# A planned two-layer kernel: another price for instruction fetch, and the value weights loaded as two halves

## The chip, the core and the metric

The kernel runs on one core of one Trainium2 chip. A core has five engines that take their instructions in order and meet only at semaphores: TensorE (PE in the profile, its weight loads PEld), VectorE (DVE), ScalarE (ACT), GpSimd (POOL) and SyncE (SP), which here only issues DMAs. The metric is the device time of one execution in microseconds; the time of a kernel is the median of its runs.

## The reference, cut to what matters

The input x is 2048 rows of 512 numbers. Two layers run one after the other, each with the same attention and the same gated block:

```python
def A(x):   # 32 heads of 16, window of 256 keys, no bias
    q, k, v = split(x @ wqkv)
    p = softmax(where(0 <= i - j < 256, q @ k.T * 16 ** -0.5, -1e9))
    return (p @ v) @ wo
def B(x):   # 512 -> 1792 -> 512
    return (sigmoid(x @ w_gate) * (x @ w_up)) @ w_down
x = x + A(layernorm(x)); x = x + B(layernorm(x))
x = x + A(layernorm(x)); x = x + B(layernorm(x))
```

The second layer uses the same weights as the first.

## The kernel before

**Tiles and stages.** The 2048 rows are 16 tiles of 128, in groups of four. For each layer and tile the stages are: layer norm (statistics L649 and L651 on VectorE, the root on GpSimd L662 and L663, the subtract-and-multiply "apply" L681 on VectorE), a transpose of the normalised tile into `xnT` (by TensorE and a copy for the first tiles, L704, otherwise as a DMA transpose of two tiles, L728), the projections of a group (queries L780, keys L811, and per tile the values L847), whose results ScalarE (L738) or VectorE (L740) copies out of a PSUM bank. The keys are then split on VectorE into even and odd halves (L826, two instructions for a quarter of the heads).

**Visits.** Attention goes in 154 visits. A tile has five: four of kind A (one for each quarter of the heads, scores at L1106) and one of kind R for the window's edges (L1117), which stands third and needs all four quarters; the last tile of a layer has two. In each, TensorE writes scores into the one PSUM tile `Sps`, ScalarE takes the exponential of 2048 columns (L1159, 1.88 us) into a ring, and VectorE multiplies masks in (L1037). The next visit's scores cannot start before ScalarE has read `Sps`. When a tile's masks are done, TensorE multiplies the probabilities with the values, in two halves of 80 small matmuls (L1186); their result is moved (L740 or L738), transposed (L1205), divided by the row sums (L1240, L1241), transposed back (L1213), multiplied with wo (L970) and added to x (L976).

**The gated block.** It works in chunks of 1, 2 or 4 tiles given by the list `GLU`: gate and up matmuls of 128, 256 or 512 columns (L875), a tanh on ScalarE (L893), a product on VectorE (L901), then 14 matmuls a tile for the down projection (L939) and the add (L948). For layer 1 the rows then go out (L955).

**What sets the order.** No scheduler of the framework is at work: class `Plan` is a list scheduler that runs while the program is built. It keeps a clock, a queue of ready tasks for VectorE, ScalarE, GpSimd and SP, and TensorE's clock; whatever the plan starts next is written next into that engine's program. Its prices are constants: a matmul of n columns takes n/2.4 + 2.5 ns, an exponential 1880, a change between kinds of matmul 100. `ARRIVE` and `RATE` say when the first loads land and how fast the later ones flow. `Plan.held` and `Plan.issue` count TensorE's instructions: for every 256 a new line is fetched, and a line is usable `LINE_NS` after the previous one was entered; when TensorE would come sooner, the plan holds it. Among several ready tasks an engine takes the one with the smallest `prio`; `rank` chooses TensorE's next unit of dense work; `pace` is the least planned time from one visit to the next. Before the change `prio`, the DMA slack, the ranks and the pace come from one table, `SEGMENTS`, with a new entry every five visits or so.

The method `pick` takes TensorE's next step: values if the plan is in them, a visit's scores if they are due, otherwise a step of a dense unit (L1338).

**The first loads.** SP and ScalarE each issue half of the first x tiles and half of the key and query weights. Then:

```python
weights("k", 1)
weights("q", 0)
self.has_wq["v"] = at("v", [first(self.wq[:, :, 2 * D:3 * D], wq_src[:, :, 2 * D:3 * D], "ACT")])
x_group(1)
self.has_wo = load(self.wot[:], wo_src, D * D * 2)
```

So the value weights go out as one DMA of 512 KB on ScalarE's queue, and x tiles 4 to 7 as two DMAs of 256 KB on SP's, beside each other. Until the first weights are there, TensorE is kept busy with dummy matmuls (L1370).

Of the kernel before, what the change touches and what calls it, by code (L numbers as in the profile page):

```python
# [12 lines left out]
P = 128  # L13
# [43 lines left out]
def pool_ns(n):  # L57
# [5 lines left out]
GLU = [[[1, 1, 1, 1, 2, 2], [1, 1, 1, 1, 2, 2], [1, 1, 2, 2, 2], [1, 1, 1, 1, 1, 1, 1, 1], [2, 2, 2, 2], [1, 1, 2, 1, 1, 2], [2, 2, 4]], [[4, 4, 4, 2, 2], [4, 4, 4, 2, 2], [4, 4, 2, 2, 4]]]  # L63
EARLY = 16
# [5 lines left out]
ARRIVE = dict(x0=3280, x1=4280, x2=5600, k=8560, q=10000, v=10900)  # L70
# [3 lines left out]
RATE = ((10900, 40.0), (1e9, 345.0))  # L74
# [3 lines left out]
LINE_NS = 3550  # L78
# [3 lines left out]
OPT = dict(gu='SP', g1=1, bk=3, bq=2, wide=0, r0=2, g0=5, g2=0, x0=1, eps=1, hold=1, own=1, ck=0, cq=2, turn=2,  # L82
    split=0, mo=0, at=3, r1=1, near=1)
RANK = dict(x3=31008.59915082838, wd=1355.5443193096523)


class Late(dict):


    def __missing__(self, name):  # L90
        return {"vv": self["v"], "tp": 0, "tp_g": 2}[name] if name in ("vv", "tp", "tp_g") else self[name[:-1]]


SEGMENTS = {
    0: (False, dict(st_x0=16.387, ap_x0=6.225, xt_x0=7.482, st_x1=3.545, ap_x1=7.915, xt_x1=12.783, st_x=12.637,
        ap_x=12.681, xt_x=-4.829, st_p=-0.616, ap_p=7.606, xt_p=5.184, st_g=-0.445, ap_g=2.621, xt_g=-2.868,
        st_g0=3.679, ap_g0=-17.463, xt_g0=-4.767, tp=8.093, tp_g=6.212, q=-2.808, q0=10.418, q1=-21.607, k=-11.975,
        k0=12.49, k1=0.894, s=-4.824, s0=2.968, s1=4.16, v=-0.758, v0=18.344, v1=21.96, vv=-1.006, exp=-7.486,
        exp0=-1.374, m0=3.414, m00=5.808, e0=-7.871, e00=2.35, e1=1.881, e10=8.977, m2=1.191, m20=5.467, th=14.916,
        mu=-10.778, dn=-19.706, add=-0.599, add0=7.919, out=-15.994, mv=30.614, mv0=7.196, oq=-9.099, oq0=-8.293,  # L100
        no=9.304, no0=-3.84, on=10.221, on0=-11.559, vc=9.867, vc0=-2.298), dict(xt=3835, oq=509, on=2499, vc=2407),
        dict(tp=-26.503, o=-3.164, lead=15.979, far=73.841, v=2.438, g=58.124, d=37.228, feed=44.486,
        x3=31008.59915082838, wd=1355.5443193096523, go=147.94192547482436), 1500.53),
    5: (False, {}, {}, {}, 1500.53),
    10: (False, {}, {}, {}, 1500.53),
    15: (False, {}, {}, {}, 1500.53),
    16: (False, {}, {}, {}, 1690.96),
    20: (False, {}, {}, {}, 1690.96),
    25: (False, {}, {}, {}, 1690.96),
    26: (True, dict(st_p=1.672, ap_p=36.822, xt_p=-2.918, st_x=-11.841, ap_x=0.6, xt_x=14.582, st_g=-13.947,  # L110
        ap_g=-7.573, xt_g=7.949, q=-14.515, k=21.982, s=1.709, v=-1.564, exp=-39.767, m0=2.485, e0=7.8, e1=8.391,
        m2=14.841, th=1.045, mu=-20.576, dn=-2.4, add=-13.535, out=27.454, mv=35.926, oq=-4.313, no=8.505, on=12.109,
        vc=-17.889), dict(xt=240, oq=3128, on=2754, vc=10020), dict(tp=36.947, o=-40.166, lead=9.199, far=17.491,
        v=-2.507, g=13.193, d=13.247, feed=-46.58, go=607.5028023985727), 2727.3),
    30: (False, dict(ap_x=1.293, dn=-2.072), dict(oq=2609), dict(feed=-47.788), 2681.58),
    35: (False, dict(st_p=0.51, ap_g=-7.3, mu=-24.39), dict(oq=2664, on=2941), dict(o=-39.26, lead=12.63, go=494),
        2681.58),
    40: (False, dict(st_p=1.672, ap_g=-7.573, mu=-20.576), dict(xt=779, oq=2609, on=2754), dict(o=-40.166,
        lead=9.199, go=607.5028023985727), 2620.7),
    45: (False, dict(st_p=0.82), dict(xt=240), dict(g=8.75, go=213), 1879.3),  # L120
    50: (False, dict(st_p=1.672), {}, dict(g=13.193, go=607.5028023985727), 2681.58),
    55: (False, {}, dict(xt=86), dict(lead=13.76), 2574.1),
    60: (False, {}, dict(xt=240), dict(lead=9.199), 2681.58),
    65: (False, {}, {}, {}, 2681.58),
    70: (False, {}, {}, {}, 2764.0),
    75: (False, {}, {}, {}, 2681.58),
    80: (False, {}, {}, {}, 2717.8),
    85: (False, dict(k=22.27, e0=8.47), {}, dict(far=18.98, v=-3.32, g=13.07), 2632.8),
    90: (False, dict(q=-15.93, k=21.982, e0=7.8, e1=11.21, add=-11.69), dict(on=2458), dict(lead=9.39, far=17.491,
        v=-2.507, g=14.8), 2717.8),  # L130
    95: (False, dict(q=-14.515, e1=8.391, add=-13.535), dict(on=2754), dict(lead=9.199, g=13.193), 2717.8),
    100: (False, {}, {}, {}, 2717.8),
    105: (False, {}, {}, {}, 2717.8),
    110: (False, {}, {}, {}, 2717.8),
    115: (False, {}, {}, dict(go=877), 2868.0),
    120: (False, {}, {}, dict(go=607.5028023985727), 2717.8),
    125: (False, {}, {}, {}, 2717.8),
    130: (False, {}, {}, {}, 2717.8),
    135: (False, {}, dict(oq=2597), dict(lead=8.49, far=16.64), 2717.8),
    140: (False, {}, dict(oq=2609), dict(lead=9.199, far=17.491), 2717.8),  # L140
    145: (False, {}, {}, {}, 2717.8),
    150: (False, {}, {}, {}, 2717.8),
}


def segments():

    out, now = {}, [Late(), {}, {}, 0]
    for slot, (new, prio, slack, rank, pace) in SEGMENTS.items():
        now = [Late(prio) if new else Late({**now[0], **prio}), {**now[1], **slack}, {**now[2], **rank}, pace]  # L150
        out[slot] = now
    return out
# [259 lines left out]
def mm_ns(n):  # L412
    return n / 2.4 + 2.5


class Net:


    def __init__(self, ctx, tc, A_x, wqkv, wo, w_gate, w_up, w_down, out):
# [39 lines left out]
        self.slot = 0  # L459

# [30 lines left out]
    def loads(self, A_x, wqkv, wo, w_gate, w_up, w_down):  # L491
# [56 lines left out]
        self.has_wq["v"] = at("v", [first(self.wq[:, :, 2 * D:3 * D], wq_src[:, :, 2 * D:3 * D], "ACT")])  # L548
# [195 lines left out]
    @property  # L744
    def prio(self):
        return self.tables[0]

    @property
    def slack(self):
        return self.tables[1]  # L750

    @property
    def ranks(self):
        return self.tables[2]

    def enter(self, slot):
        self.slot = slot
        if slot in self.segments:
            self.tables = self.segments[slot]
# [11 lines left out]

    def q_unit(self, L, g, cq, i0, n):
# [6 lines left out]
        def steps(bank):  # L779
            return [(mm_ns(w), lambda kt=kt, o=o: nc.tensor.matmul(  # L780
                self.banks[bank][:, o:o + w], lhsT=self.wq[:, kt, cq * P:cq * P + P],
                rhs=self.xnT[key][0][:, i0 + o // P:i0 + (o + w) // P, kt, :],
                start=kt == 0, stop=kt == KT - 1)) for o in range(0, n * P, w) for kt in range(KT)]
# [19 lines left out]
    def k_unit(self, L, g, cq, i0, n):  # L803
# [6 lines left out]
        def steps(bank):  # L810
            return [(mm_ns(w), lambda kt=kt, o=o: nc.tensor.matmul(  # L811
                self.banks[bank][:, o:o + w], lhsT=self.wq[:, kt, D + cq * P:D + cq * P + P],
                rhs=self.xnT[key][0][:, i0 + o // P:i0 + (o + w) // P, kt, :],
                start=kt == 0, stop=kt == KT - 1)) for o in range(0, n * P, w) for kt in range(KT)]
# [27 lines left out]
    def v_unit(self, L, t):  # L842
# [3 lines left out]
        def steps(bank):  # L846
            return [(mm_ns(D), lambda kt=kt: nc.tensor.matmul(  # L847
                self.banks[bank][:], lhsT=self.xnT[key][0][:, t % NBG, kt, :], rhs=self.wq[:, kt, 2 * D:3 * D],
                start=kt == 0, stop=kt == KT - 1)) for kt in range(KT)]
# [17 lines left out]
    def glu_units(self, L, t0, n, c0):  # L867
# [5 lines left out]
        def mms(bank, wts, fcs):  # L873
            pt = self.banks[bank][:, 0:len(wts) * len(fcs) * w].rearrange("p (i f w) -> p i f w", i=len(wts), w=w)
            return [(mm_ns(w), lambda i=i, j=j, fc=fc, wt=wt, kt=kt: self.nc.tensor.matmul(  # L875
# [52 lines left out]
    def down_units(self, L, t, t0, n, c0):  # L928
# [4 lines left out]
        def unit(o, w):  # L933
# [3 lines left out]
            def mm(bank, fc):  # L937
                at = (c0 * GW + fc * n * P + (t - t0) * P) % (HCH * GW)
                nc.tensor.matmul(self.banks[bank][:, 0:w], lhsT=self.hT[:, at:at + P], rhs=self.wd[:, fc, d],  # L939
                                 start=fc == 0, stop=fc == FC - 1)  # L940
                if t == t0 + n - 1 and end:
                    pl.at(pl.pe_free + PE_LATENCY, self.h_used[L, t0, fc].fire)
# [23 lines left out]
    def oproj_unit(self, L, t, b):  # L966
        nc, pl = self.nc, self.pl

        def steps(bank):
            return [(mm_ns(D), lambda c=c: nc.tensor.matmul(  # L970
# [312 lines left out]
    def pick(self):  # L1283
# [23 lines left out]
        if visit and pl.mode == "pv" and go <= 0:  # L1307
            if go > 0:
                return False
# [6 lines left out]
        if visit and (wait <= 0 or go <= 0 and u is None):  # L1316
            self.last_s = pl.now
            end = pl.matmul("s", self.scores(*visit))
# [5 lines left out]
            self.enter(self.slot + 1)  # L1324
# [14 lines left out]
        pl.count(1)  # L1339
        end = pl.matmul("d", ns)  # L1340
# [8 lines left out]

    def do_values(self, pv, spare):  # L1350
        pl = self.pl
        self.pv_list.pop(0)
        bank = min(spare, key=lambda i: self.bank_turn[i])
# [20 lines left out]
    def pace(self, s):  # L1374
        return self.tables[3] if s < len(self.visits) else 0
# [111 lines left out]
    def go(self, *srcs):  # L1487
        pl = self.pl
        self.visit_list()
        self.segments = segments()  # L1490
        self.enter(0)
# [23 lines left out]
        self.v_needs = [self.visit_needs(*v) for v in self.visits]  # L1515
        self.last_s = -1e9
# [80 lines left out]
```

## Time and profile before

| | us |
|---|---|
| median of 3 runs | 540.27 (539.95 to 540.88) |
| the profiled execution: its time | 541.94 |
| the profiled execution: its span | 540.2 |
| PE busy | 523.8 (97% of the span), 9606 matmuls recorded |
| PE weight loads busy | 292.6 (54%) |
| VectorE busy | 417.6 (77%) |
| ScalarE busy | 385.0 (71%) |
| GpSimd busy | 43.5 (8%) |
| DMA of data issued by SP: share of the 16 engines | 31.9% |
| mean granted TensorE clock | 1.00 |

The span is the stretch from the first to the last instruction of the profiled execution; its time has some more around it. Busy times overlap, since the engines work beside each other. A row of the groups or of the timeline names line, engine, operation and tiles; a bracket or an arrow tells how long the engine stood idle before it and what ended that. The chain follows the instruction that ended last back to what released it, step by step. The program has 9674 matmuls; some of them are missing in the records.

### The profile page before, as it was taken

Reading aid. Unit: us, or ns where it says so; the run is one execution under the profiler, and the core shown is the slowest. Engines: PE = TensorE matmul, PEld = TensorE weight load, DVE = VectorE, ACT = ScalarE, POOL = GpSimd, SP = SyncE. Lnnn points to the kernel's source line nnn. Section 1 sums busy time; section 2 is a strip of 40 time slices with the busy share of each in tenths; the row PEclk is TensorE's granted clock in tenths of the full one; section 3 lists DMA queues with packets and bytes.
Section 4 is the critical chain, followed back from the end, with each engine's and each line's share of the span. In section 5 each row is a group of like instructions: output and inputs, shape, how many; then the busy total and the mean of one; then the engine's idle time right before and its main releaser. Section 6 shows DMA issues by size and latency. Waiting matters only on the chain.

```text
span 540.2 us, 21309 instructions
## 1 busy us (share of the span) xinstructions
PE 523.8 (97%) x9606; PEld 292.6 (54%) x9674; DVE 417.6 (77%) x841; ACT 385.0 (71%) x384; POOL 43.5 (8%) x99
## 2 busy tenths in 40 slices
PE   8899999999999999999999998999999999999997
PEld 8446855758657544544444444444444454445873
DVE  6999989898798897779896988789886774442442
ACT  4999988979889797789688887688877751220330
POOL 4411200000001010000110100100000000000000
PEclk9999999999999999999999999999999999999999
DMA  8851433234223327225235325342143224101001
GB/s 261 311 155 52 81 82 42 59 68 80 43 52 42 72 41 93 46 59 72 47 51 72 51 54 48 65 60 63 32 81 52 51 42 69 39 1 38 3 11 39
DMA packets 95067, 36.23 MB, mean 67 GB/s; under 512 B 78336, under 2 KB 93952, under 8 KB 94976
## 3 DMA queue, kind: packets, MB, share of 16 engines
q1 hardware_dynamic: 93600, 33.56, 31.9%
q8 instruction: 75, 1.23, 1.0%
q10 hardware_dynamic: 1376, 1.31, 0.8%
q14 instruction: 16, 0.13, 0.1%
HBM read 9.70 MB, written 2.10 MB: 22 GB/s over the span
## 4 chain that ended last, share of the span: by engine, by line
PE 86%; DMA 4%; DVE 4%; ACT 3%; issue 2%; ACTq 0%; SPq 0%; DVEq 0%
PE bank L875 34%; PE bank L939 17%; PE bank L1186 9%; PE Sps L1106 7%; PE bank L970 5%; PE bank L847 4%; PE bank L811 4%; PE bank L780 4%; DMA xnT<-xn 2%; PE Sps L1117 2%; DMA xsb<-in_A_x_dram 1%; ACT edge L1159 1%; DMA wq<-in_A_wqkv_dram 1%; ACT PTring L1159 1%; DVE st L649 0%
## 5 line engine op out<-in xcount | busy, mean ns | idle before, releaser
L1159 ACT ACTIVATE PTring<-Sps 128x2048 bf16<-128x2048 f32 (+1 forms) x122 | 226.1, 1853 | 45.3 <-PE Sps L1106 41.8
L875 PE MATMUL bank<-xnT,wu 128*128 128x512 bf16 (+2 forms) x728 | 128.6, 297 | 0.1
L875 PE MATMUL bank<-xnT,wg 128*128 128x512 bf16 (+2 forms) x728 | 127.8, 298 | 0.2 <-issue 0.2
L901 DVE SCALAR_TENSOR_TENSOR hT<-hT,bank 128x256 bf16<-128x256 bf16 (+1 forms) x154 | 80.7, 538 | 50.8 <-ACT hT L893 26.3
L893 ACT ACTIVATE hT<-bank 128x256 bf16<-128x256 f32 (+1 forms) x154 | 71.4, 483 | 68.1 <-PE bank L875 67.0
L939 PE MATMUL bank<-wd,hT 128*128 128x512 bf16 (+2 forms) x429 | 101.8, 372 | 3.2 <-issue 2.4
L875 PEld LDWEIGHTS <-wg 128*128 128x128 bf16 x728 | 61.2, 98 | 37.4 <-issue 2.7
L875 PEld LDWEIGHTS <-wu 128*128 128x128 bf16 x728 | 61.9, 98 | 34.6 <-issue 1.9
L939 PEld LDWEIGHTS <-hT 128*128 128x128 bf16 x462 | 42.5, 98 | 47.0 <-issue 1.9
L1159 ACT ACTIVATE edge<-Sps 128x2048 bf16<-128x2048 f32 (+1 forms) x32 | 56.6, 1770 | 13.9 <-PE Sps L1117 13.4
L1186 PE MATMUL bank<-PTring,Vaug 128*32 128x64 bf16 (+1 forms) x2880 | 51.8, 203 | 1.4 <-issue 1.4
L1186 PEld LDWEIGHTS <-Vaug 128*32 128x32 bf16 x2880 | 44.1, 97 | 13.0 <-issue 11.2
L1037 DVE TENSOR_TENSOR PTring<-PTring,mask 128x1024 bf16<-128x1024 bf16 x64 | 43.6, 684 | 7.8 <-ACT PTring L1159 7.7
L740 DVE CAST OTs<-bank 128x512 bf16<-128x512 f32 x52 | 37.8, 728 | 14.0 <-PE bank L1186 13.8
L1106 PE MATMUL Sps<-qT,kTp 32*128 32x256 bf16 (+3 forms) x1216 | 47.4, 248 | 0.8 <-ACT edge L1159 0.4
L649 DVE BATCH_NORM_STATS2 st<-xsb 128x6 f32<-128x512 bf16 x64 | 44.0, 687 | 2.5 <-DMA xsb<-in_A_x_dram 1.8
L1186 PE MATMUL bank<-edge,Vl 128*32 128x64 bf16 x1024 | 44.6, 193 | 0.0
L662 POOL TENSOR_SCALAR st<-st 128x2 f32<-128x2 f32 (+1 forms) x33 | 11.2, 339 | 412.6 <-DVE st L651 412.6
L1106 PEld LDWEIGHTS <-kTp 32*128 32x128 bf16 x1216 | 17.8, 92 | 43.0 <-issue 40.9
L1037 DVE TENSOR_TENSOR edge<-edge,maske 128x1024 bf16<-128x1024 bf16 x60 | 39.9, 681 | 1.2 <-ACT edge L1159 1.0
L1186 PE MATMUL bank<-edge,Vh 128*32 128x64 bf16 x896 | 40.7, 193 | 0.0
L1037 DVE TENSOR_TENSOR PTring<-PTring,maskn 128x1024 bf16<-128x1024 bf16 x56 | 38.2, 682 | 1.7 <-ACT PTring L1159 1.7
(75 smaller groups left out, 523.3 us busy)
## 6 DMA issues: line engine op xcount, KB each, us to landing
Vl<-Vaug SPq DMA_DIRECT2D x32, 68.0 KB, 2.4
out_dram<-xsb SPq DMA_DIRECT2D x15, 128.0 KB, 2.1
Vh<-Vaug SPq DMA_DIRECT2D x28, 68.0 KB, 2.3
wg<-in_B_w_gate_dram SPq DMA_DIRECT2D x2, 896.0 KB, 10.1
wu<-in_B_w_up_dram SPq DMA_DIRECT2D x2, 896.0 KB, 10.7
wd<-in_B_w_down_dram SPq DMA_DIRECT2D x7, 256.0 KB, 3.2
xsb<-in_A_x_dram SPq DMA_DIRECT2D x6, 256.0 KB, 7.2
wq<-in_A_wqkv_dram SPq DMA_DIRECT2D x2, 256.0 KB, 4.7
```

The lines of the kernel that those rows point to most:

```text
L649: nc.vector.bn_stats(out=st[:, 0:6], in_=self.xsb[:, t, :])
L740: self.nc.vector.tensor_copy(out=out, in_=in_)
L780: return [(mm_ns(w), lambda kt=kt, o=o: nc.tensor.matmul(self.banks[bank][:, o:o + w], lhsT=self.wq[:, kt, cq * P:cq * P + P], rhs=self.xn ...
L875: return [(mm_ns(w), lambda i=i, j=j, fc=fc, wt=wt, kt=kt: self.nc.tensor.matmul(pt[:, i, j, :], lhsT=wt[:, kt, fc * P:(fc + 1) * P], rhs= ...
L893: self.nc.scalar.activation(out=self.hT[:, ch[0] * GW:ch[0] * GW + size], in_=pt, func=AF.Tanh, scale=0.5)
L901: self.nc.vector.scalar_tensor_tensor(out=h, in0=h, scalar=1.0, in1=pt, op0=ALU.add, op1=ALU.mult)
L939: nc.tensor.matmul(self.banks[bank][:, 0:w], lhsT=self.hT[:, at:at + P], rhs=self.wd[:, fc, d], start=fc == 0, stop=fc == FC - 1)
L970: return [(mm_ns(D), lambda c=c: nc.tensor.matmul(self.banks[bank][:], lhsT=b[0][:, c, :], rhs=self.wot[:, c, :], start=c == 0, stop=c == ...
L1037: done = pl.task({"DVE": dve_bf_ns(1024)}, lambda e: nc.vector.tensor_tensor(out=r, in0=r, in1=m.to_broadcast([P, 16, HP]), op=ALU.mult), ...
L1106: nc.tensor.matmul(self.sps[:, m, o:o + n * HP], lhsT=kTp[32 * m:32 * m + 32, i, tt, e, :], rhs=self.qT[32 * m:32 * m + 32, i, q0:q0 + n * ...
L1159: nc.scalar.activation(out=out, in_=src, func=AF.Exp, scale=scale)
L1186: nc.tensor.matmul(o, lhsT=Va[:, c0:c0 + 32], rhs=p(h), start=k == 0 or t == 0, stop=k == len(parts) - 1 or t == 0, tile_position=(0, 32 * g))
```

## The change

The prices that the planner reckons with are changed: `LINE_NS` from 3550 to 4500, the planned arrival of v from 10.9 to 11.9 us, of x2, k and q by 0.04 to 0.1 us, and the moment from which later loads flow from 10.9 to 11.6. The table by segments is replaced by two sets of priorities, slacks and ranks with other values: one up to visit 24, one from there on. The pace becomes 1514 ns for the first 16 visits, 56 up to visit 24, then 2675 in layer 0 and 2422 in layer 1 (before: 1501, then 1691, then mostly 2682 and 2718). Two entries of `GLU` change: the chunks of layer 0 are tiles 0, 1, 2-3, 4-5, 6-7, 8-11, 12-15 (before, 4 and 5 stood alone), and layer 1 has four chunks of four (before, the last four tiles were 2 and 2).

The value weights are loaded as two halves of 256 KB, one on ScalarE's queue and one on SP's, and the SP half stands ahead of the x group. A helper `mm` issues most matmuls; it can split one into four column strips, which `OPT["col"] = 0` switches off.

Since the planner makes every engine's order anew from these numbers, the order of the instructions differs on all engines from about the first scores on. TensorE has 9450 matmuls instead of 9674, all of the difference in gate and up. SP has one DMA more. VectorE's and ScalarE's work is the same but for the gated block's chunks and for which of the two makes a copy.

```diff
-GLU = [[..., [1, 1, 2, 1, 1, 2], [2, 2, 4]], [[4, 4, 4, 2, 2], [4, 4, 4, 2, 2], [4, 4, 2, 2, 4]]]
+GLU = [[..., [1, 1, 2, 2, 2], [2, 2, 4]], [[4, 4, 4, 4], [4, 4, 4, 4], [4, 4, 4, 4]]]
+PACE = [2674.92, 2421.83, 1514.06, 55.78, 24.82]
...
-ARRIVE = dict(x0=3280, x1=4280, x2=5600, k=8560, q=10000, v=10900)
+ARRIVE = dict(x0=3280, x1=4280, x2=5500, k=8600, q=9900, v=11900)
...
-RATE = ((10900, 40.0), (1e9, 345.0))
+RATE = ((11600, 40.0), (1e9, 345.0))
...
-LINE_NS = 3550
+LINE_NS = 4500
...
-SEGMENTS = {
...
-}
+PRIO = dict(st_x0=11.96, ap_x0=1.481, xt_x0=15.743, st_x1=4.799, ap_x1=4.987, xt_x1=17.198, st_x=11.858,
...
+SLACK = dict(xt=4114, oq=705, on=2212, vc=3028)
...
+LATE_PRIO = dict(st_p=1.209, ap_p=39.706, xt_p=-8.546, st_x=-19.015, ap_x=12.134, xt_x=28.172,
...
+LATE_SLACK = dict(xt=145, oq=2215, on=3133, vc=11347)
...
-        self.has_wq["v"] = at("v", [first(self.wq[:, :, 2 * D:3 * D], wq_src[:, :, 2 * D:3 * D], "ACT")])
+        weights("v", 2)
...
+    def mm(self, out, lhsT, rhs, start, stop):
+        if not self.col:
+            self.nc.tensor.matmul(out, lhsT=lhsT, rhs=rhs, start=start, stop=stop)
+            return
...
     def pace(self, s):
-        return self.tables[3] if s < len(self.visits) else 0
+        if s >= len(self.visits):
+            return 0
+        if s < PACE[4]:
+            return PACE[2 if s < EARLY else 3]
+        return PACE[self.visits[s][0]]
```

The halves come from a function that was there for the key and query weights:

```python
def weights(name, i):
    h = slice(i * D, i * D + D)
    self.has_wq[name] = at(name, [first(self.wq[:, k:k + 2, h], wq_src[:, k:k + 2, h], q) for k, q in ((0, "ACT"), (2, "SP"))])
```

## The prediction

> **What bounds the kernel now.** I read the page's busy times and chain first, then the chain in order of time, the waits, and the timeline of the first 75 us.
>
> ```profile
> span 540.2 us, 21309 instructions
> PE 523.8 (97%) x9606; PEld 292.6 (54%) x9674; DVE 417.6 (77%) x841; ACT 385.0 (71%) x384; POOL 43.5 (8%) x99
> ...
> PE 86%; DMA 4%; DVE 4%; ACT 3%; issue 2%; ACTq 0%; SPq 0%; DVEq 0%
> ```
>
> TensorE is busy for 97% of the span and is 86% of the chain: the order of its instructions is the time, plus whatever it waits. The chain in order of time gives the prices:
>
> ```profile
> 57.19 2.45 PE bank L875 x42
> ...
> 64.84 0.81 PE bank L1186 x80
> ...
> 283.13 4.55 DMA xnT<-xn
> ...
> 336.26 1.35 issue
> ...
> 352.98 5.01 DMA xnT<-xn
> ...
> 465.41 3.45 PE bank L875 x16
> ...
> 497.78 3.49 PE bank L875 x32
> ```
>
> So a matmul of 512 columns costs 216 ns (3.45/16), of 256 columns 109 (3.49/32), of 128 some 57 (2.45/42), a half of the values 0.81 us; a visit's scores cost 0.33 us (chain pieces at L1106). Where a run of wide matmuls ends and scores or values begin, start to start is 312 ns instead of 216: 0.1 us a change. Adding these up in the order of the built program gives 526.9 us. The span has 13.3 us more: 3.8 by the first scores (12.96 in the trace, 9.2 in the sum), 3.2 behind the last matmul (the last stretch, from 530.0, has 6.95 us of PE), and 6.3 of waits between. Those 6.3 are all that a better order can win. Where they lie:
>
> ```profile
> 14.11 0.69 DVE L649 BATCH_NORM_STATS2 st<-xsb 128x6 f32<-128x512 bf16 x1 [0.82 <-DMA xsb<-in_A_x_dram]
> ...
> 18.15 1.58 DVE L826 TENSOR_SCALAR kTp<-kTp,rm 128x512 bf16<-128x512 bf16 x4
> ...
> 19.78 0.33 PE L1117 MATMUL Sps<-qT,kTp 32*128 32x64 bf16 x20 [0.66 <-DVE kTp L826]
> ```
>
> ```profile
> 59.57 0.41 PE L1117 MATMUL Sps<-qT,kTp 32*128 32x64 bf16 x32
> ...
> 60.06 1.88 ACT L1159 ACTIVATE edge<-Sps 128x2048 bf16<-128x2048 f32 x1
> ...
> 61.99 0.40 PE L1106 MATMUL Sps<-qT,kTp 32*128 32x256 bf16 x8 [0.40 <-ACT edge L1159]
> ```
>
> The first shows VectorE idle for 0.82 us until the second group of x is there, and TensorE then waiting for VectorE's key splits (with the wait at 18.91, 1.24 us). The second shows the exponential's cycle: scores at 59.57, ScalarE until 61.94, next scores at 61.99, so 2.42 us from visit to visit at the least. At visit 22 (72.8 us) the trace is 7.1 us behind the sum, 3.3 more than at the first scores; from there to the end only 2.9 are added: 1.35 at 336.26 inside one run of values ("issue": nothing the profile shows), about 1.1 at the two DMA pieces above, the rest in tenths.
>
> **The change, part by part.** (1) *TensorE's own work.* Tiles 4 and 5 of layer 0 go from two chunks of one tile to one of two, tiles 12 to 15 of layer 1 from 2+2 to 4. The first trades 224 matmuls of 128 columns for 112 of 256: 112 x (2x57 - 109) = -0.5 us. The second trades 224 of 256 for 112 of 512: 112 x (2x109 - 216) = -0.2. The order has 379 runs instead of 374, five more changes at 0.1: +0.5. Dummy matmuls are 80 in both. The helper that now issues the matmuls has its split switched off. Sum -0.2 us.
>
> (2) *The head.* SP issues one more DMA (about 0.65 us, the spacing of its neighbours) ahead of the x group, so both x halves, the output weights and all behind them go out one place later. Before, the two x halves landed at 10.6 and 14.0 and the whole value block on ScalarE's queue at 14.5 (issued at 4.20, 10.3 us to landing). TensorE's first value matmul is at 17.11, so the earlier value weights win nothing. x is now last of the same bytes on the same DMA engines: I put it at 14.0 to 14.5, take 14.35, +0.3. The Trainium skill, "DMA: Bandwidth & Descriptors", section "Issuing engines are not separate DMA queues", says that DMAs issued by several engines run on the same 16 DMA engines and that a second queue saves only issue time, which speaks against this part; v and x landing half a microsecond apart agree with it, and by it x comes no sooner and the sum is 542.2 us, where halves at twice the rate would make it 539.5.
>
> What matters more: in VectorE's new order the statistics of tiles 4 and 5 (which wait for x) stand ahead of the second key split, where before they stood behind it. Visit 1 needs that split. By rows: statistics from 14.44, 1.71 us for two tiles (14.11 to 15.82 before), split 0.81 (1.62 for two), so visit 1's scores start at 17.0, not 15.46: 1.5 us late. Everything on TensorE stands behind them: the first transposes of tile 4, the last keys, the values. Then VectorE does an apply 0.4, statistics 0.87, an xnT copy 0.41, a split 0.81 and a qT copy 0.68, until 20.15; the first value unit wants that copy's bank, and TensorE would be there at 18.9: 1.3 more, together 2.8. In exchange visit 2 (R) stands one unit further back, and its 1.24 us of waits at 18.91 and 19.78 go; its lag behind the sum becomes 6.65 instead of 5.5. Net +1.2 us. Ends: x at 12.5 takes both waits away and leaves the gain, -1.5; x at 15.0 gives +1.9.
>
> (3) *Visits too close together.* Between successive scores the new order leaves 1.74, 2.17, 1.98 and 1.75 us of TensorE's work (visits 4, 7, 9, 15); the cycle is 2.42: 0.68 + 0.25 + 0.44 + 0.67 = 2.0 us of waits. Before there were 2.29 and 1.95: 0.6. Net +1.4; ends 0 (other waits fall into the same gaps) and +2.0.
>
> (4) *Hand-over between stages.* From the last down matmul of a group to its first queries the chain by rows is: matmul 0.38, add 0.69, statistics 0.69 + 0.18, GpSimd 0.34 + 0.76, apply 0.81, DMA transpose 3.7 (median) to 5.0: 7.5 to 8.9 us. For tiles 8 to 11 before layer 1's queries the new order has 7.5 us of work between (14.4 before), so 0 to 1.4, take 0.6; for the gate work of tiles 8 to 11 in layer 0 it has 8.3 (9.5), take 0.3. For tiles 12 to 15 it has 16.4 (12.6), so the wait at 358 goes. Set against the 1.1 that the trace has now: -0.2; ends -1.1 and +2.0.
>
> (5) *Instruction fetch.* The planner now counts 4,500 ns for 256 instructions. The trace's instruction packets come 3.5 us apart at the closest and TensorE stood 1.35 us once. But the new order has as many places as the old one where two value halves stand back to back (three runs of 160), the densest there are. So I give half of the 1.35 back: -0.7; ends -1.4 and +1.4. The Trainium skill, "Runtime: NRT & Kernel Launch", section "Instruction fetch mechanics", calls the cost of crossing a 16 KiB block mostly hidden; by it this term is 0 and the sum 0.7 higher.
>
> (6) *Closer visits in layer 1.* Most stand 2.54 to 2.60 us apart (2.76 to 2.81 before), with one gap of 14.2 that is full of gate and down work. VectorE is 85% busy there now (42.4 of 50 us from 350 to 400) and has 7% less time per visit; late masks would hold the values up. +0.4; ends 0 and +2.0.
>
> Sum: -0.2 + 1.2 + 1.4 - 0.2 - 0.7 + 0.4 = +1.9 us on the profiled execution, whose time was 541.94 for a span of 540.2; the median is 1.67 below it, so 540.27 + 1.9 = 542.2 us.
>
> **Rivals.** *x lands early.* By the trace's packets 15 of the 16 parts of v were through by 11.9 us and one lagged until 14.0. If the halves spare x that laggard, VectorE never waits for it and the head is -1.5 instead of +1.2: 542.2 - 2.7 = 539.5, not slower. It decides from the point where x lands more than 1.5 us earlier than before. Against it: the load and the laggard are the same. *Close visits are free.* ScalarE is 96% busy from 30 to 45 us and may be the bound there in both orders, so that the gaps of TensorE's work below 2.42 us cost nothing: 542.2 - 1.4 = 540.8, no change. For it: ScalarE's total work is nearly the same. Against it: TensorE idles only 0.6 us of the 30 from 30 to 60, so its own work sets the pace now. With both, 538.1: faster. *Much slower.* Layer 1 has no slack: four groups whose transposes take 5.0 instead of 3.7 us, and values that wait for masks, 4 x 1.3 less the 1.3 counted: 542.2 + 3.9 = 546.1. For it: both transposes on the chain took 4.55 and 5.01; against: the gap of 14.2. *The change doesn't do what it says*: the longer fetch shows nowhere in the density, so (5) gives nothing back: 542.9, inside the likeliest's range.
>
> **How the numbers follow.** Likeliest 0.48 (540.8 to 544.5 by its own), x early alone 0.10, close visits free alone 0.11, both 0.12, much slower 0.19. Below 538.6 and above 546.0 I leave a tenth each. What a measurement can tell is 0.2%, 1.1 us: faster is below 539.2, slower above 541.35. Faster is both (0.12) and the lower part of x early: 0.15. Same is the rest of these two and the lowest part of the likeliest: 0.20. Slower is what is left, 0.65.
>
> **What would show it.** In the new profile: VectorE idle for over 1 us before the first statistics of tile 4 near 14.4; scores of visit 1 near 17.0; a wait of the first value unit for a qT copy near 20; scores waiting for the exponential some 0.4 to 0.7 us about visits 5, 10 and 16; visit 22 near 75 us. PE busy within 1 us of 523.8. At 290 to 300 us a wait for xnT under 1.5 us. It is wrong if x lands early, if one wait above 2 us stands in layer 1, or if the run of values at 336 has more than one successor.

## The result, and the profile after

The changed kernel takes 542.2 us (median of 7 runs, 541.58 to 542.85); the kernel before, on the same chip, 540.49 (7 runs, 539.95 to 540.96). The ratio is 1.0025 with a 95% interval of 1.0015 to 1.0034: slower by a quarter of a per cent, 1.7 us. The forecast was 542.2. The number fits, its terms don't: the terms added 1.6 us too much to the time of the profiled execution (541.94 + 1.9 = 543.8, the new profile's is 542.25), and the last step, from the profile down to the median, took off as much too much. That they cancel is luck.

The page of the changed kernel, its span, busy times and chain by engine:

```profile
span 540.5 us, 20853 instructions
...
PE 525.2 (97%) x9382; PEld 280.2 (52%) x9450; DVE 413.9 (77%) x828; ACT 383.9 (71%) x369; POOL 42.7 (8%) x99
...
PE 86%; DVE 7%; ACT 4%; issue 2%; DMA 1%; POOL 0%; ACTq 0%
```

TensorE is still 97% busy and 86% of the chain. The chain of the kernel before had 4% DMA and 4% DVE, this one has 1% and 7%. The share of DVE is no loss by itself: the fastest kernel of this study (run 9 below) has 7% there too. The chain in order of time of the changed kernel, from 285 to 375 us, shows the two pieces that answer to the DMA and "issue" pieces shown for the kernel before:

```profile
294.98 3.08 DMA xnT<-xn
...
321.36 0.52 issue
```

One transpose on the chain instead of two, and 0.52 us in which TensorE waited for nothing that the profile shows, instead of 1.35. So far this is what was forecast. The head is not. The timeline of the changed kernel, first 21 us:

```profile
12.65 0.69 DVE L608 BATCH_NORM_STATS2 st<-xsb 128x6 f32<-128x512 bf16 x1
...
14.27 0.71 DVE L788 TENSOR_SCALAR kTp<-kTp,rm 128x512 bf16<-128x512 bf16 x2
...
15.78 0.40 PE L1068 MATMUL Sps<-qT,kTp 32*128 32x256 bf16 x8
...
18.53 1.67 PE L728 MATMUL bank<-wq,xnT 128*128 128x512 bf16 x6 [0.71 <-DVE qT L699]
...
20.13 0.41 PE L1079 MATMUL Sps<-qT,kTp 32*128 32x64 bf16 x32
```

The statistics of tile 4 start at 12.65 with no idle time before them: x was there already. The second key split comes at 14.27 and visit 1 at 15.78, not at 17.0. The wait for the qT copy is where it was expected, but 0.71 us long instead of 1.3. From then on the close visits show, in the timeline of the changed kernel from 24 to 58 us:

```profile
27.68 0.40 PE L1068 MATMUL Sps<-qT,kTp 32*128 32x256 bf16 x8 [0.57 <-ACT PTring L1121]
...
41.51 0.40 PE L1068 MATMUL Sps<-qT,kTp 32*128 32x256 bf16 x8 [0.54 <-ACT PTring L1121]
...
43.21 0.40 PE L663 MATMUL bank<-ident,xn 128*128 128x128 bf16 x4 [0.33 <-DVE xn L640]
...
56.09 0.40 PE L663 MATMUL bank<-ident,xn 128*128 128x128 bf16 x4 [0.24 <-DVE xn L640]
...
57.02 0.21 PE L1148 MATMUL bank<-PTring,Vaug 128*32 128x64 bf16 x4 [0.30 <-DVE PTring L999]
```

Scores wait for the exponential at visits 5 and 10 (27.68 and 41.51), as forecast. Behind visit 10 (43.21) and ahead of visit 16 (56.09 and 57.02) TensorE waits for VectorE's apply and mask, which was not forecast.

The measure used below is the *lag* of the prediction: the start of a visit's scores in the trace, less the sum of the rows of TensorE's program up to it (the row "sum of rows" is worked out from the prediction's prices and the built program, not measured). The kernel before has two columns, since the fourth run profiled it once more; the fifth and sixth column are two experiments told below (runs 9 and 10).

| lag, us | before, as predicted from | before again | after | chunks alone | chunks and close visits |
|---|---|---|---|---|---|
| visit 0 | 3.79 | 4.30 | 4.11 | 3.90 | 3.92 |
| visit 3 | 5.75 | 5.02 | 5.01 | 4.61 | 4.63 |
| visit 22 | 7.05 | 6.40 | 8.34 | 5.99 | 7.94 |
| last matmul | 9.81 | 8.55 | 9.74 | 6.57 | 9.25 |
| sum of rows | 526.92 | 526.92 | 526.84 | 526.86 | 526.85 |
| from there to the end of the span | 3.47 | 3.46 | 3.88 | 3.45 | 3.46 |

### The profile page after: what moved, and what is told of

Its sections match the earlier page's. It is cut to its first block, busy times and chain, and to the rows that moved or that the text cites. A ratio compares the mean times of both kernels' runs of the same rounds, so it can differ in the third digit from the quotient of the medians.

```text
span 540.5 us, 20853 instructions
## 1 busy us (share of the span) xinstructions
PE 525.2 (97%) x9382; PEld 280.2 (52%) x9450; DVE 413.9 (77%) x828; ACT 383.9 (71%) x369; POOL 42.7 (8%) x99
## 3 DMA queue, kind: packets, MB, share of 16 engines
q8 instruction: 74, 1.21, 1.0%
## 4 chain that ended last, share of the span: by engine, by line
PE 86%; DVE 7%; ACT 4%; issue 2%; DMA 1%; POOL 0%; ACTq 0%
PE bank L728 68%; PE bank L1148 8%; PE Sps L1068 6%; ACT PTring L1121 2%; PE Sps L1079 2%; ACT edge L1121 1%; PE bank L1338 1%; DVE PTring L999 1%; DVE kTp L788 1%; DVE st L608 1%; DVE edge L999 1%; DVE qT L699 1%; DMA xnT<-xn 1%; DVE kTp L699 0%; DVE xsb L938 0%
## 5 line engine op out<-in xcount | busy, mean ns | idle before, releaser
L728 PE MATMUL bank<-xnT,wu 128*128 128x512 bf16 (+2 forms) x616 | 125.0, 321 | 0.0
L855 ACT ACTIVATE hT<-bank 128x512 bf16<-128x512 f32 (+1 forms) x140 | 69.6, 513 | 72.4 <-PE bank L728 71.6
L863 DVE SCALAR_TENSOR_TENSOR hT<-hT,bank 128x512 bf16<-128x512 bf16 (+1 forms) x140 | 78.7, 575 | 52.2 <-PE bank L728 42.7
L728 PE MATMUL bank<-wd,hT 128*128 128x512 bf16 (+2 forms) x427 | 103.2, 372 | 3.2 <-issue 2.2
L728 PEld LDWEIGHTS <-wu 128*128 128x128 bf16 x616 | 54.5, 98 | 40.9 <-issue 2.7
L728 PEld LDWEIGHTS <-wg 128*128 128x128 bf16 x616 | 53.6, 98 | 41.5 <-issue 2.3
L728 PE MATMUL bank<-xnT,wq 128*128 128x512 bf16 (+1 forms) x316 | 63.2, 339 | 0.3 <-DMA xnT<-xn 0.3
L699 DVE CAST OTs<-bank 128x512 bf16<-128x512 f32 x45 | 32.6, 728 | 13.4 <-PE bank L1148 13.4
```

The costliest lines, as they stand in the source:

```text
L699: self.nc.vector.tensor_copy(out=out, in_=in_)
L728: self.nc.tensor.matmul(out, lhsT=lhsT, rhs=rhs, start=start, stop=stop)
L855: self.nc.scalar.activation(out=self.hT[:, ch[0] * GW:ch[0] * GW + size], in_=pt, func=AF.Tanh, scale=0.5)
L863: self.nc.vector.scalar_tensor_tensor(out=h, in0=h, scalar=1.0, in1=pt, op0=ALU.add, op1=ALU.mult)
```

## The experiments

**1 and 2: the halves, undone and alone.** TensorE's order is the same in each pair, so only the loads differ.

```diff
 (1, from the changed kernel; 2 is the reverse in the kernel before)
-        weights("v", 2)
+        self.has_wq["v"] = at("v", [first(self.wq[:, :, 2 * D:3 * D], wq_src[:, :, 2 * D:3 * D], "ACT")])
```

> The changed kernel with the value weights loaded as one block of 512 KB on ScalarE's queue again, everything else as changed; TensorE's order is the same instruction for instruction. Theory (the halves brought x early): the first statistics of tile 4 fall back from 12.65 to about 14.1 us with VectorE idle over 1 us, visit 1 starts near 17 instead of 15.78, visit 2 is over 1 us later, and the time rises from 542.2 to 543 to 544 us. Rival (x's landing has nothing to do with the halves, a lagging DMA engine comes and goes by itself): statistics of tile 4 below 13 us, visit 1 at 15.8, time 542.2.

> The kernel before with the value weights as two halves, nothing else; TensorE's order is that of the kernel before. Theory: x lands near 12.6 us, VectorE's idle 0.82 us at 14.11 and some of TensorE's 1.24 us of waits for key splits at 18.91 and 19.78 go; the lag behind the sum of rows at visit 3 falls from 5.75 to 4.5 to 5.2 us and the time from 540.5 to 539.3 to 540.0. Rival (the key splits wait for something else than VectorE's place behind the statistics): waits unchanged, 540.5.

Run 1: 542.59 us, ratio to the kernel before 1.0038 (1.0024 to 1.0051), beside 1.0025 (1.0015 to 1.0034) with halves: the intervals overlap. Its timeline:

```profile
12.69 0.69 DVE L608 BATCH_NORM_STATS2 st<-xsb 128x6 f32<-128x512 bf16 x1
```

Statistics at 12.69, no idle time, visit 1 at 15.77: x is as early with one block as with halves. The rival holds. Run 2: 541.1 us, ratio 1.0007 (0.9998 to 1.0015): the halves win nothing in the old order either, though in its profile, too, the waits for key splits are down from 1.24 us to one of 0.44 at 18.89.

The fourth run says why: most of that wait was not the order's.

**4: the kernel before, profiled again.** No edit.

> The kernel before, unchanged, profiled once more. Theory (the 1.35 us in which TensorE stood inside a run of values at 336 us belongs to that one execution): no gap over 1 us there, a span near 538.8 us, a time of 540 to 541. Rival (it belongs to the order): 1.2 to 1.5 us at the same place, and a span near 540.

540.68 us, span 538.9. From its timeline, two rows of the head and two of the late part:

```profile
13.72 0.69 DVE L649 BATCH_NORM_STATS2 st<-xsb 128x6 f32<-128x512 bf16 x1
...
19.08 0.33 PE L1117 MATMUL Sps<-qT,kTp 32*128 32x64 bf16 x20 [0.21 <-ACT qT L738]
...
287.28 0.61 PE L780 MATMUL bank<-xnT,wq 128*128 128x512 bf16 x2 [0.92 <-DMA xnT<-xn]
...
336.46 0.21 PE L1186 MATMUL bank<-PTring,Vaug 128*32 128x64 bf16 x2 [0.64 <-issue]
```

In the head the statistics follow without idle time, and of the 1.24 us of waits 0.21 are left, for a copy by ScalarE (in runs 2 and 6, of the same order, one wait for a key split of 0.44 and 0.43 us stays). The late x belonged to the one execution that the prediction was worked out from: there the second half of x tiles 4 to 7 landed at 14.02 us, in 12 others of the 14 profiles of this study at 11.68 to 12.85 (in run 2 it isn't recorded), and it is the only one in which VectorE waits over 0.2 us there. The theory on the stall at 336 us, however, falls: it is there again, 0.64 us long. In the profiles of runs 2 and 6, which have the same order, it is 1.08 and 1.10. It belongs to the order, with a length that varies.

**3: the changed kernel with the early tables of the kernel before.**

```diff
-ARRIVE = dict(x0=3280, x1=4280, x2=5500, k=8600, q=9900, v=11900)
+ARRIVE = dict(x0=3280, x1=4280, x2=5600, k=8560, q=10000, v=10900)
-RATE = ((11600, 40.0), (1e9, 345.0))
+RATE = ((10900, 40.0), (1e9, 345.0))
-PACE = [2674.92, 2421.83, 1514.06, 55.78, 24.82]
+PACE = [2674.92, 2421.83, 1500.53, 1690.96, 24.82]
-SLACK = dict(xt=4114, oq=705, on=2212, vc=3028)
+SLACK = dict(xt=3835, oq=509, on=2499, vc=2407)
...
```

(PRIO and RANK likewise take the values of the first segment of the kernel before.)

> The changed kernel with the planner's early set (priorities, slacks, ranks, arrivals and pace up to visit 24) of the kernel before; halves, chunks, fetch price and the set from visit 24 on stay as changed. TensorE's order up to visit 17 is then that of the kernel before; its rows sum to 527.2 instead of 526.8. Theory (the change loses in the first 75 us, where visits stand closer than the exponential's 2.42 us): the shortfalls up to visit 24 go from 2.1 to 0.4 us, the lag at visit 22 from 8.34 to 6 to 7 us, and the time to 540 to 541. Rival (the loss lies in layer 1, in its closer visits or in the hand-over between stages): lag at visit 22 smaller, but the end no earlier, 542 us.

540.37 us, ratio 0.9995 (0.9986 to 1.0004): the loss is gone. The lag at visit 22 is 5.98 instead of 8.34. TensorE's waits from 20 to 73 us (engine and line, what it waited for: us in total, times, longest), first of the changed kernel:

```profile
PE Sps L1068 <- ACT PTring L1121: 1.1, 2, 0.6
PE bank L663 <- DVE xn L640: 0.6, 2, 0.3
PE bank L728 <- issue: 0.3, 2, 0.2
PE bank L1148 <- DVE PTring L999: 0.3, 1, 0.3
PE Sps L1068 <- ACT edge L1121: 0.2, 1, 0.2
```

and of the third run:

```profile
PE bank L728 <- issue: 0.5, 3, 0.2
PE Sps L1068 <- ACT PTring L1121: 0.3, 1, 0.3
PE Sps L1068 <- ACT edge L1121: 0.2, 1, 0.2
PE bank L1215 <- DVE OTs L699: 0.2, 1, 0.2
```

The waits for ScalarE fall from 1.3 to 0.5 us, those for VectorE from 0.9 to 0.2.

**5 and 6: a shorter exponential in visits 10 to 23**, in the changed kernel and in the kernel before, to see how much of the loss is ScalarE's cycle.

```diff
-        x = pl.task({"ACT": EXP_NS}, lambda e: self.exp(L, t, kind, i), ...
+        x = pl.task({"ACT": EXP_NS}, lambda e: self.exp(L, t, kind, i, 10 <= s < 24), ...
...
+        if short and kind == "A":
+            out, src = out[:, 0:6], src[:, 0:6]
+        elif short and kind == "R" and t > 2:
+            out, src = out[:, :, 0:1], src[:, :, 0:1]
         nc.scalar.activation(out=out, in_=src, func=AF.Exp, scale=scale)
```

> The changed kernel with a shorter exponential in visits 10 to 23: six of eight heads of a kind-A visit, one edge of two of a kind-R visit from tile 3 on (the rest is left out, so part of the attention isn't computed; four small memsets on GpSimd stand in); TensorE's order is the same. Theory (scores wait for ScalarE to have read the score tile where visits stand closer than the exponential's cycle): the cycle falls from 2.42 to about 2.0 us, the 0.9 us lost between visits 15 and 16 (1.75 us of work between them) fall to 0.2 to 0.3, lag growth from visit 10 to 22 falls from 1.5 to about 0.8 us, time 541.4 to 541.8. Rival (the loss there is VectorE's masks or copies, which are the same): growth stays 1.5, time 542.2.

> The kernel before with the same shorter exponential in visits 10 to 23. Theory: only the gap between visits 17 and 18 (1.95 us of work) is below the cycle, so 0.4 to 0.5 us are won; lag growth from visit 10 to 22 falls from 0.9 to 0.4 or 0.5; time 540.6 to about 540.2. Rival: growth stays 0.9 and the time 540.6.

Run 6: lag growth from visit 10 to 22 is 0.56 instead of 0.90, the wait before visit 18 is gone, 540.3 us: ratio 0.9993 (0.9984 to 1.0002). The profile shows what the theory had; the time alone can't tell it from no gain. Run 5: 542.51 us, ratio 1.0036 (1.0023 to 1.0048); lag growth 1.28 instead of 1.50, where the theory wanted 0.8. Between visits 15 and 16 0.79 us are still lost of 0.89. From its timeline:

```profile
55.91 1.45 ACT L1127 ACTIVATE PTring<-Sps 128x1536 bf16<-128x1536 f32 x1 [0.58 <-PE Sps L1070]
...
57.31 0.22 PE L1154 MATMUL bank<-PTring,Vaug 128*32 128x64 bf16 x4 [0.30 <-DVE PTring L1001]
```

ScalarE is done at 57.36 now, and idles 0.58 us before; TensorE stands behind VectorE all the same, in the middle of the values, for a mask. So the theory fails for visit 16. For visits 5 and 10 it rests on the waits in the timeline alone: run 5 leaves the exponentials ahead of them as they were, and the wait at visit 10 stays 0.54 us. Where visits stand close, VectorE's work for them stands close too, and at visit 16 it was VectorE that ended the wait.

**8: the old price for instruction fetch.**

```diff
-LINE_NS = 4500
+LINE_NS = 3550
```

> The changed kernel with the planner's price for a line of TensorE's instructions back at 3,550 ns; TensorE's order up to visit 19 is the same, later parts differ, the rows sum to 527.17 instead of 526.84. Theory (the price buys nothing on the chip, the 1.35 us stall of the kernel before was one execution's): lag at the end 9.5 to 10.0 us as now, the time 0.3 us longer by the sum, 542.2 to 542.6. Rival (the higher price prevents stalls): one or more stalls of 1 to 1.5 us inside a run of values, time 543 to 545.

542.17 us, ratio 1.0021 (1.0012 to 1.0029), beside 1.0025 with the new price. The price is worth nothing that can be measured, and the stall of TensorE is there with both: 0.52 us at 321.88 in the changed kernel (0.53, 0.31 and 0.66 in runs 1, 5 and 11, which have its order), 0.38 at 321.24 here.

**9 and 10: the chunks alone in the kernel before, and with them the close visits.** Run 10 adds to run 9 the changed early set (PRIO, SLACK, RANK, ARRIVE, RATE and the pace up to visit 25).

```diff
 (9)
-GLU = [[..., [1, 1, 2, 1, 1, 2], [2, 2, 4]], [[4, 4, 4, 2, 2], [4, 4, 4, 2, 2], [4, 4, 2, 2, 4]]]
+GLU = [[..., [1, 1, 2, 2, 2], [2, 2, 4]], [[4, 4, 4, 4], [4, 4, 4, 4], [4, 4, 4, 4]]]
```

> The kernel before with the changed chunks of the gated block alone (layer 0: tiles 4 and 5 together; layer 1: four chunks of four). TensorE's order up to visit 24 is that of the kernel before, the rows sum to 526.86 (526.92 before), SP has 328 instructions as before. Theory (the chunks are worth nothing but their rows): 540.4 to 540.9. Rival (fewer, wider matmuls ease the fetch or the hand-over between stages): 539.0 to 539.8.

> The run before this one with the changed early set (priorities, slacks, ranks, arrivals, pace up to visit 25) put into the kernel before, the value weights still one block; TensorE's order up to visit 18 is then that of the changed kernel, later parts are those of the old tables; rows sum to 526.85, SP has 331 instructions. Theory (the changed kernel loses in its first 75 us): lag at visit 22 of 8.2 to 8.6 instead of 6.4, and a time 1.3 to 2.0 us above the run with the chunks alone. Rival (the early loss is made up later, since the late part has slack): within 0.5 us of it.

Run 9: 539.38 us (538.66 to 539.76), ratio 0.9976 (0.9966 to 0.9986). It beats both kernels, by 1.0 and 2.8 us. The theory fails, its rival holds. TensorE's longest waits in it:

```profile
PE bank L939 <- issue: 2.2, 14, 0.2
PE bank L1370 <- DVE hT L565: 1.0, 1, 1.0
PE bank L970 <- issue: 0.5, 3, 0.2
PE Sps L1106 <- ACT edge L1159: 0.4, 1, 0.4
```

and in the kernel before, fourth run, with the two entries that run 9 has no more:

```profile
PE bank L780 <- DMA xnT<-xn: 0.9, 1, 0.9
PE bank L1186 <- issue: 0.6, 1, 0.6
```

The wait for `xnT` at 287 us and the stall at 336 are both gone, and no other took their place. That these two are worth the whole 1.0 us is read from the profile, not shown by a run of its own: the chunks change the order of everything behind visit 24.

Run 10: 541.9 us, ratio 1.0028 (1.0016 to 1.0040). The early set alone costs 2.5 us against run 9. The lag grows by 3.31 us from visit 3 to 22 (3.33 in the changed kernel) instead of 1.38, and nothing of it comes back later. Run 3 takes the set away from the changed kernel and wins 1.8 us (542.2 to 540.37). Together they settle that the changed kernel loses by its early set, most of it ahead of visit 22; which of the set's constants do it, pace or priorities, wasn't tried.

**7, 11 and 12: the end of SP's program.** The changed kernel takes 0.4 us longer from its last matmul to the end of the span, in runs 1, 3, 5 and 8 as well. All of these have 341 to 343 instructions on SP. Run 7 is run 3 with the last stores on another engine, run 11 is the changed kernel with those of four earlier tiles there, run 12 is run 7 with the old fetch price.

```diff
 (7; in 11: nc.scalar if 8 <= t < 12)
-                    pl.dma(640, P * w * 2, lambda: nc.sync.dma_start(out=dst, in_=self.xsb[:, t, d]), ...
+                    pl.dma(640, P * w * 2, lambda: (nc.scalar if t >= 12 else nc.sync).dma_start(out=dst, in_=self.xsb[:, t, d]), ...
```

> The changed kernel with the early set of the kernel before (as in the third run), and the output stores of tiles 12 to 15 issued by ScalarE instead of SyncE, which takes SP from 341 instructions to 331; TensorE's order is that of the third run. Theory (SP stands for some 0.36 us at one fixed instruction, about the 336th of its program, which the kernel before with 328 never reaches): the stretch from the last matmul to the end of the span falls from 3.97 to 3.4 to 3.6 us, the time from 540.4 to about 540.0, below the kernel before. Rival (the tail hangs on the stores themselves): 3.9 us and 540.4, or more, if a store from ScalarE lands later.

> The changed kernel with the output stores of tiles 8 to 11 issued by ScalarE; those of the last four tiles stay on SP. TensorE's order is the same; SP has 335 instructions instead of 343. Theory (SP stands at one fixed instruction of its program near the end): the stretch from the last matmul to the end of the span falls from 3.88 to about 3.5 us, the time by 0.3 to 0.5 us, to 541.7 to 541.9. Rival (in the earlier run the stores on ScalarE did it): 3.9 us and 542.2.

> Early set and fetch price of the kernel before, halves, chunks and late set as changed, the last four tiles' stores on ScalarE (SP 334 instructions). Rows sum to 526.85, 0.3 less than in the run with the early set and the stores. Theory: 539.7 to 540.1, 0.4 to 1.0 below the kernel before. Rival (what the sum gains, other waits take): 540.1 to 540.6.

| kernel | SP instructions | last matmul to end, us |
|---|---|---|
| before, runs 4, 6, 9 | 328 | 3.45 to 3.47 |
| run 2 | 329 | 3.52 |
| runs 10, 7, 12, 11 | 331, 331, 334, 335 | 3.46, 3.54, 3.56, 3.52 |
| runs 3, 1 | 341, 342 | 3.97, 3.90 |
| after, runs 5, 8 | 343 | 3.88, 3.89, 3.90 |

There is a step between 335 and 341 instructions, and it doesn't matter which stores were moved: run 11 keeps the last ones on SP. Run 7: 540.09 us, ratio 0.9993 (0.9984 to 1.0001), beside 0.9995 in run 3; run 11: 541.62, ratio 1.0022 (1.0013 to 1.0031), beside 1.0025. The tail shows the step clearly, the times only lean the same way.

The traces show where it comes from. In the changed kernel SP stands 0.33 us between its 335th and its 336th recorded instruction (539.25 to 539.58 us; two of its 343 are not recorded). In runs 1, 3, 5 and 8 it stands 0.33 to 0.36 us at the very same count, though in run 3 other instructions are there, and the programs with at most 335 end before it.

Whether a fetch of instructions is behind it stays open. The changed kernel has 16 packets on the second instruction queue (q14 on its page), run 11 has 15; but run 5 has 15 too, with the long tail, and run 12 has 16 with the short one. The page counts only what starts within the span, and in the changed kernel the last packet is recorded at 540.22, after SP went on.

Run 12: 540.61 us, ratio 1.0001 (0.9993 to 1.0010): the rival. The better sum is taken by other waits, of which two stand in its timeline:

```profile
203.33 0.21 PE L1148 MATMUL bank<-PTring,Vaug 128*32 128x64 bf16 x4 [0.54 <-DVE PTring L999]
...
204.81 0.59 PE L728 MATMUL bank<-xnT,wg 128*128 128x512 bf16 x2 [0.72 <-DMA xnT<-xn]
```

## Why the prediction was right in its number and wrong in its terms

By its own steps, on the two profiled executions that it speaks of (spans of 540.2 and 540.5 us), in us:

| step | predicted | found | what the runs show |
|---|---|---|---|
| (1) TensorE's rows | -0.2 | -0.1 (sum of rows) | right, not measured apart |
| (2) head, to visit 3 | +1.2 | -0.7 | wrong |
| (3) close visits, visit 3 to 22 | +1.4 | +2.0 | place right, too small, about half of it another engine |
| (4) + (5) + (6), behind visit 22 | -0.5 | -1.4 | too small; (5) near in size, wrong in cause |
| tail | not in the sum | +0.4 | missed |
| sum | +1.9 | +0.3 | |

*(1)* is right by the sum over the built programs (526.92 to 526.84). Its price of 57 ns for 128 columns is slightly off: 2.45/42 is 58, and start to start the trace of the kernel before has 56 in the median, which takes the first trade from -0.5 to -0.3. PE's busy time rose by 1.4 us, outside the 1 us that was given for it; the busy time counts modelled ends, the sum of rows doesn't.

*(2) failed* at "I put it at 14.0 to 14.5, take 14.35". What made x late in the one profile was taken for a property of the load, but x landed so late in 1 of 14 profiles. "It is wrong if x lands early" was the prediction's own sign, and it came true: x's second half landed at 11.94 us, statistics began at 12.65 without idle time, visit 1 stood at 15.78. With x early in both, the head is even: lag 5.02 and 5.01 at visit 3. What was argued from the trace's packets under the rival "x lands early" did come about, but not by the halves (run 1), and the kernel before has it too (runs 4 and 6). So the rule that was weighed there, of the Trainium skill's "DMA: Bandwidth & Descriptors", section "Issuing engines are not separate DMA queues", agrees with runs 1 and 2: two queues brought x no sooner (its second half landed at 11.94 to 12.85 us in the seven profiles with halves that record it, at 11.68 to 12.55 in five of the six with one block, and at 14.02 in the sixth).

*(3)* named visits 5, 8, 10 and 16 and the waits 0.68, 0.25, 0.44 and 0.67; the lag grows there by 0.63, 0.25, 0.61 and 0.89, and visit 22 starts at 73.1 us, not near 75. But the last is VectorE's (run 5), and 0.50 more about 43.21 is, by the timeline, VectorE's as well, which the working had no term for: it counted the gaps on TensorE against ScalarE's cycle alone. Against run 4 the growth is 1.95 us more than in the kernel before, against run 9 in run 10 1.93. The rival "close visits are free" is out: runs 3 and 10 give the early set a price of 1.8 and 2.5 us.

*(4) and (5)*: in the two profiles the stall goes from 1.35 to 0.52 us, -0.83 where -0.7 was said, and the waits for `xnT` from 0.94 to 0.28. The 1.35 was the longest of four in that order (0.64, 1.08, 1.10 in runs 4, 2 and 6), and the changed order has 0.31 to 0.66, so about half a microsecond is the order's and the rest chance. But the price of a fetch has no part in it (run 8), so the rival that the change doesn't do what it says was true of its first half. What takes both waits away is an order that comes with the chunks (run 9). The stall is there again in the changed kernel and in runs 1, 5, 8 and 11, where the changed early and late sets stand together, and in none of runs 3, 7, 10 and 12, which have only one of the two: neither set brings it by itself. *(6)* shows nowhere: behind visit 22 no wait of TensorE for VectorE is longer than 0.2 us in the changed kernel.

*The last step* hid all this: "the median is 1.67 below it, so 540.27 + 1.9". The profiled execution of the kernel before was slow by things of its own, its late x and its long stall: against run 4 its lag is 0.7 us higher at visit 3 and 1.3 at the end. A change cannot be set against these and the usual distance to the median kept as well. Between the two profiles the change is +0.3 us; between medians +1.7. The new profile is 0.05 us above its median, not 1.67: this step took off 1.6 us too much, just what the terms had added too much. The forecast's number is right by that luck. Worked out against run 4 the terms would be: rows -0.1, head 0.0, close visits +1.95, behind visit 22 -0.75, tail +0.4, together +1.5, which is the difference of the medians within 0.2.

By medians the parts are: chunks -1.0 (run 9), early set +2.5 (run 10 against 9), together +1.5 of the 1.7. All the rest, halves, price, late set and SP's longer program, adds nothing that can be told to run 10: it has a ratio of 1.0028, the changed kernel 1.0025. But the parts don't simply add: beside the old early set the same rest costs about 1.0 us (run 3, 0.9995, against run 9, 0.9976), and the early set, taken away there, is worth 1.8 and not 2.5. What of the rest does it wasn't taken apart.

## What to carry to other kernels

Before a forecast is worked out from one profile, look for what in it might be that execution's own (a transfer that ends on one late packet, a stall with no cause in the trace): take it out of the base, or out of the step from the profile to the median, but don't count it in both. When visits or blocks move closer together, count the shortfall for every engine that works per visit, not only for the one with the longest instruction. And try a change of many constants part by part: here one part alone, the chunks, was worth 1.0 us, and another cost 1.8 to 2.5.

## What the runs showed of the hardware

TensorE's stalls without a cause in the trace stand at one place of its program's raster. Counted in the built programs, the stall near 336 us is before instruction 14,019 to 14,021 in the kernel before and in runs 2, 4 and 6, the one near 322 before 13,250 to 13,252 in the changed kernel and runs 1 and 11 (some matmul records are missing, so the count may be off by two). Run 6 has one more, 0.44 us at 138.58, before instruction 5,827. Divided by 256, all of these leave 194 to 197. The page of the changed kernel gives 74 packets and 1.21 MB for TensorE's instruction queue, 16 KB each; its 18,914 instructions are 73.9 times 256:

```profile
q8 instruction: 74, 1.21, 1.0%
```

So the stalls stand a whole number of packets apart in the program; read so, TensorE stands where a new packet of its instructions begins, 0.3 to 1.35 us long, in 9 of 14 profiles; in the other 5, which have other orders, no wait "issue" over 0.2 us stands behind the head. The Trainium skill's "Runtime: NRT & Kernel Launch", section "Instruction fetch mechanics", calls the cost of such a crossing mostly hidden: that fits most crossings of these programs, and not these. Why it is one crossing of 74, nearly always the same in an order, stays open; that TensorE comes to it through two halves of values back to back fits the kernel before, not the changed one, where it stands within scores.

SP shows something alike: at one count of its program, near the 336th instruction, it stood 0.33 to 0.36 us in all five profiles that reach it, and as that falls behind the last store, the tail is 0.4 us longer (table above). That it is a fetch as well is not shown.
